# Input loads of a fused FFT-mixing and ELU kernel: row cuts, gather spacing, the read of channel 128

## The chip, the core and the metric

The kernel runs on one core of one Trainium2 chip. The metric is the device time of one execution in microseconds; the median of three runs of the kernel before is 1978.52 us (1977.29 to 1978.53). Nothing else runs on the chip.

The core has five engines with an instruction stream each: PE (matmul), DVE (vector), ACT (activation functions, copies), POOL (general elementwise, gathers) and SP (issues DMAs). A DMA is issued by SP, ACT or POOL and carried out by the core's 16 DMA engines. An engine executes its stream in order, so an instruction that waits holds up all that stand behind it.

## The reference

```python
X = np.fft.fft(x, axis=1)          # x: (8, 3008, 256)
X = np.fft.fft(X, axis=2).real
h = X.reshape(24064, 256) @ w_in   # (256, 2048)
g = np.where(h > 0.0, h, np.exp(np.minimum(h, 0.0)) - 1.0)
out = g @ w_out                    # (2048, 256)
```

The real part of the two-dimensional transform of a real x is C x C' - S x S', with cosine and sine matrices along the sequence (C, S) and the channels. It is even under a flip of both axes. The kernel therefore transforms half of the sequence, 1504 columns a batch, and gets the rows k and 3008 - k of the output from the sum and the difference of the same two products. The transform along the channels is multiplied into w_in on the chip, once.

## The kernel before, in words

**Columns, tiles, steps.** There are 8 x 1504 = 12032 columns in 47 tiles of 256 (TW). A tile takes 8 steps, 376 in all; each step handles two blocks of 128 of the 2048 hidden channels. A batch is 47 steps. In a step PE computes P (`mm_P`, H<-Rr,Wc) and Q (`mm_Q`, H<-Ir,Ws), DVE adds channel 128 between them (`even_part`, L960, E<-Rb,wex,H), ACT and DVE form the ELU of h plus and h minus, POOL forms four sums of the results (`sum_1`, `sum_3`, `sum_2`, `sum_4`, all through `gtt`, L484), and PE multiplies by w_out in seven products (`mm_X1`, `mm_X2`, `mm_X3` into pA to pD; pB's second product, from WT, needs `sum_2`). The first two tiles use the plain form without sums, since POOL is then converting weights. Results are transposed on DVE and stored by SP (`store`, L1191), up to 16 DMAs a transposed half.

**Input.** The sequence transform of a batch starts from folds: rows s, 3008 - s, 1504 - s and 1504 + s are brought onto the same partition, so that sums and differences can be formed (`fold_x`, L572: e0 to e3, o0 to o3, then E0, E2, EO0 and so on). `load_x` fills four tiles L[0] to L[3] (named xl) of 128 partitions x 6 rows of 256 channels. Each holds three pairs of rows, of which one kind runs forward at the pace of 8 rows a partition and comes by plain DMAs (`runs`, L238, queue SP, or ACT for most loads of the first batch), and the other is read backward through six gathers on POOL (`gather`, L217), whose row numbers stand in the table `ix` (`row_tables`, L189). The table RUNS cuts the 128 partitions where the row number jumps: at 96, 94 or 64. In the last batch one gather is followed by a repair (L228) of one row that would lie past the end of x; it is issued on POOL into the same tile.

**The rest of the start.** Weights come as 64-bit floats and are converted on DVE, ACT and POOL in chunks (`Chunk`: a, b, p, l, d, R, s, M, P are its operations; raw loads at L283), and folded with the channel transform on PE (f0 and so on). `load_mats` brings the transform matrices MC. PE starts with 46 matmuls on zeros.

**Channel 128** has no partner in the flip and is treated apart: `load_ext` (L806) reads it for all batches, 4 bytes a row, in 50 DMAs, already sorted into the order of the folds, through a DRAM tensor (xe_dr, L829) and back over 128 partitions (`get_ext`, L837: tile xs); `fold_ext` (POOL) and `dft_ext` (PE, H<-MC,xe) follow, and `spread_ext` broadcasts the result to Rb. `spread_last_row` (L524, L527) sends the matching row of each weight chunk through DRAM into wex.

**Order.** The order of most work on each engine is written out by hand: `at(t, fn)` puts a piece at a planned time, in units where a step is T = 4.8, and all pieces are issued in the order of t; FRONT lists the pieces of the first steps by name. What is wrapped in `pin` keeps this order on its engine. Plain DMAs outside `pin` are placed on their queue by a planner, by when their data are ready in its own estimate. SP's DMAs use eight semaphores in turn (the trace shows the numbers 100, 102 and 104 to 109): one that reuses a semaphore waits until the DMA before on it has landed. Each of the tiles xl has one buffer, so a load of the next batch waits until the folds have read the last one.

**Lines that the change touches:** RUNS (L120), `row_tables` (L175), `gather` (L211), `runs` (L232), the list of loads (L243), the entry `ops["x1", 0]` of `fold_x`, `load_ext` and `get_ext`, the first calls after the warm-up matmuls, and the times of `load_ext`, `get_ext` and the gathers:

```python
for n in range(24):
    at((14.4 + 0.33 * n) * T, lambda n=n: load_ext(*divmod(n, 6)))
at(30.0 * T, get_ext)
...
    l0, gap = (s0 - 8, 1) if b > 1 else (3.2, 0.5)      # s0 = 47 (b - 1)
    t = l0 + gap * n / 1.5 if n < 6 else l0             # gather n of batch b
```

Of the kernel before, what the change touches and what calls it, by code (L numbers as in the profile page):

```python
# [9 lines left out]
FP = mybir.dt.float32  # L10
# [5 lines left out]
ALU = mybir.AluOpType  # L16

SEQ = 3008
ND = 256
# [92 lines left out]
def _pick_consts():  # L112
# [6 lines left out]

RUNS = (  # L120
    (0, 0, 96, 0, 8),
# [9 lines left out]
def kernel(  # L131
# [42 lines left out]

    def row_tables():  # L175

        for c, first, n, base in (
            (1, 0, 128, 750),
            (1, 96, 32, 250),
            (0, 0, 128, HALF - 1),  # L180
            (0, 96, 32, HALF - 501),
            (2, 0, 128, HALF - 5),
            (2, 64, 64, HALF - 259),
            (3, 0, 128, HALF - 1),
            (3, 96, 32, HALF - 501),
            (3, 0, 1, HALF - 2),
        ):
            pin(
                nc.gpsimd.iota(  # L189
                    ix[first : first + n, c : c + 1],  # L190
                    pattern=[[0, 1]],
                    base=base,
                    channel_multiplier=-8,
                )
            )
            if c == 1 and first:
                pin(
                    nc.vector.tensor_scalar(
                        out=ix[:, 1:2], in0=ix[:, 1:2], scalar1=0x3FF, scalar2=None,
                        op0=ALU.bitwise_and,  # L200
                    )
                )

    def load_x(b):

        L = [
            spool.tile([128, 6 * ND], FP, tag=f"xl{j}", bufs=1, name=f"xl{j}")
            for j in range(4)
        ]

        def gather(j, pair):  # L211
            back = j in (1, 2)
            cut = b == NB - 1 and j == 1 and pair == 0
            c = 3 if cut else pair
            block = 2 - pair if back else pair
            pin(
                nc.gpsimd.indirect_dma_start(  # L217
                    out=L[j][:, 2 * block * ND : (2 * block + 2) * ND],
                    out_offset=None,
                    in_=xflat,  # L220
                    in_offset=bass.IndirectOffsetOnAxis(
                        ap=ix[:, c : c + 1].bitcast(U32), axis=0
                    ),
                    element_offset=(b * SEQ + (HALF if j in (1, 3) else 0)) * ND,
                )
            )
            if cut:
                nc.gpsimd.dma_start(  # L228
                    out=L[1][0:1, 4 * ND : 5 * ND], in_=xrows(b, SEQ - 1, 1, 1, 1)
                )  # L230

        def runs(j, queue=nc.sync):  # L232
            back = j in (1, 2)
            for pair, p, q, r, step in RUNS:
                if back != (pair == 1):
                    continue
                row = (0, SEQ, HALF, HALF)[j] + (-r - 1 if back else r)
                queue.dma_start(  # L238
                    out=L[j][p:q, 2 * pair * ND : (2 * pair + 2) * ND],
                    in_=xrows(b, row, 8, q - p),  # L240
                )

        loads = [  # L243
            lambda j=j, pair=pair: gather(j, pair)
            for j, pair in ((3, 1), (2, 0), (2, 2), (0, 1), (1, 0), (1, 2))
        ]
        loads += [lambda j=j, **kw: runs(j, **kw) for j in (3, 2, 0, 1)]
        return L, loads
# [213 lines left out]
    nc.vector.memset(zero, 0.0)  # L462
    row_tables()
    r128_dr = dpool.tile([NB, HALF], FP, tag="r128", name="r128")
# [100 lines left out]

    def fold_x(L, engine_of, cuts_of):

# [12 lines left out]
        for j in range(4):  # L580
# [21 lines left out]
            O.append(o)  # L602
        ops["x1", 0] = lambda: act(L[1][0:1, 5 * ND :], L[0][0:1, 0:ND])
        op("E0", E[0], E[0], E[1], ALU.add)
# [188 lines left out]

    def load_ext(j, run):
        if j == 0 and run == 0:
            state["x1"] = spool.tile([128, HALF + 1], FP, tag="rx", bufs=1, name="x1")
        t = state["x1"][j * NB : (j + 1) * NB, 0:768].rearrange(
            "b (p m) -> b p m", m=6
        )
        pair, p, q, s, step = RUNS[run]  # L800
        back = j in (1, 2)
        row = (0, SEQ, HALF, HALF)[j] + (-s if back else s)

        def copy(m, p, q, row):
            pin(
                nc.sync.dma_start(  # L806
                    out=t[:, p:q, m : m + 1],
                    in_=bass.AP(
                        tensor=xt,
                        offset=x.offset + row * ND + 128,  # L810
                        ap=[
                            [SEQ * ND, NB],
                            [(-step if back else step) * ND, q - p],
                            [1, 1],
                        ],
                    ),
                )
            )

        with nc.allow_non_contiguous_dma(reason="one channel"):  # L820
            for o in range(2):
                first = row + (-o if back else o)
                if first == SEQ:
                    copy(0, 0, 1, 0)
                    copy(0, 1, q, first - step)
                else:
                    copy(2 * pair + o, p, q, first)
        if run == len(RUNS) - 1:
            nc.sync.dma_start(  # L829
                out=xe_dr[j], in_=state["x1"][j * NB : (j + 1) * NB, 0:768]  # L830
            )

    def get_ext():
        xs = state["xs"] = spool.tile([128, 4, NB, 6], FP, tag="xs", bufs=1, name="xs")
        with nc.allow_non_contiguous_dma(reason="short runs"):
            for j in range(4):
                nc.sync.dma_start(  # L837
                    out=xs[:, j], in_=xe_dr[j].rearrange("b (p m) -> p b m", m=6)
                )

# [418 lines left out]
    L_first, loads = load_x(0)  # L1259
    for load in loads[:7]:  # L1260
        load()
    for load in loads[7:]:
        load(queue=nc.scalar)
    exp_neg(warm)
    w1_chunks[0].load()
    nc.sync.dma_start(out=CC, in_=CC_dr.ap())
# [270 lines left out]
    def begin_folds(b):  # L1537
        state["EO"], state["ops"] = fold_x(
            state["L"], lambda key: nc.gpsimd, lambda key, n: (0, n) if n == 128 else (0, n // 2, n)
        )  # L1540
# [7 lines left out]
    at(11 * T + 3.6, lambda: spread_ext(0, 1))  # L1548
    for n in range(24):
        at(  # L1550
            (14.4 + 0.33 * n) * T,
            lambda n=n: load_ext(*divmod(n, 6)),
        )
    at(30.0 * T, get_ext)
    at(32 * T + 1.35, fold_ext)
# [11 lines left out]
    for b in range(1, NB):  # L1567
        s0 = (b - 1) * steps_b
        late = 2 if b == 1 else 0
        l0, gap = (s0 - 8, 1) if b > 1 else (3.2, 0.5)  # L1570
        if b > 1:
            at(l0 * T + 0.1, lambda b=b: open_x(b))
        for n in range(10):
            t = l0 + gap * n / 1.5 if n < 6 else l0
            if b > 1:
# [74 lines left out]
```

## Time and profile before

| | |
|---|---|
| median of three runs | 1978.52 us |
| the profiled execution | 1980.33 us, its span 1978.5 us |
| PE busy | 1935.5 us (98%) |
| POOL, DVE, ACT busy | 1403.5, 1316.0, 862.6 us |
| granted PE clock, whole span; 15.3 to 35.6 us | 0.99; 0.50 |
| DMA | 69.69 MB; 262269 packets, of which 245534 under 512 bytes |
| first P matmul (step 0) | 43.15 us |
| steps 0 to 375 | the rest, about 5.1 us each |

Times are from the start of the span. A row of a group of instructions names line, engine, operation, output<-input and count. "L475", "L481", "L484" and "L487" are the helpers through which every matmul, DVE tensor operation, POOL operation and ACT function goes, so these are told apart by their tiles. The idle time at the end of a row is that of the engine ahead of the instruction, with what ended it. The busy time of PE includes the warm-up and the matmuls at half clock. A queue named SPq or ACTq shows issue time, not transfer; where several issues are merged into one row, its duration includes the waits between them.

### The profile page before, as it was taken

To read this page: it belongs to the slowest core of one execution; us is meant where nothing else is said; L and a number is where in the kernel's file an instruction comes from. 1 tells how busy PE (TensorE), PEld (TensorE's weight loads), DVE (VectorE), ACT (ScalarE), POOL (GpSimd) and SP (SyncE) were. 2 spreads that over 40 slices of the span, in tenths; PEclk is the share of its full clock that TensorE was granted. 3 is DMA by queue.
4 is the path that set the end of the run, shared out by engine and by line. 5 is a ranking of instruction groups with operands and counts; after the bars stand their busy time and mean duration, and the time that the engine had idled before them with its cause. 6 is when DMAs were issued, how large, how long until landed. Compare 5 with 4: busy or idle time off the path is not lost.

```text
span 1978.5 us, 27318 instructions
## 1 busy us (share of the span) xinstructions
PE 1935.5 (98%) x8912; PEld 1656.1 (84%) x8912; DVE 1316.0 (67%) x2517; ACT 862.6 (44%) x1671; POOL 1403.5 (71%) x1869
## 2 busy tenths in 40 slices
PE   6999999999999999999999999999999999999999
PEld 3788778888888888888888888888878888888887
DVE  5876566667666666667666666666656666667666
ACT  2654344444444443444444444444434444444443
POOL 2788666787678776887677776778766787555665
PEclk7999999999999999999999999999999999999999
DMA  8315320110111111111111112102020000100101
GB/s 265 93 21 31 40 60 14 28 47 16 43 16 36 33 21 48 17 40 22 30 43 20 34 22 50 22 19 50 14 54 11 20 15 19 19 11 12 22 9 24
DMA packets 262269, 69.69 MB, mean 35 GB/s; under 512 B 245534, under 2 KB 246450, under 8 KB 262128
## 3 DMA queue, kind: packets, MB, share of 16 engines
q1 hardware_dynamic: 255496, 54.06, 14.6%
q0 software_dynamic: 3872, 12.59, 2.0%
q10 hardware_dynamic: 2760, 1.31, 0.3%
q8 instruction: 70, 1.15, 0.3%
q14 instruction: 71, 0.58, 0.1%
HBM read 43.07 MB, written 24.80 MB: 34 GB/s over the span
## 4 chain that ended last, share of the span: by engine, by line
PE 88%; DVE 4%; DMA 3%; POOL 2%; SPq 1%; issue 1%; ACT 0%; ACTq 0%; DVEq 0%; POOLq 0%
PE H L475 35%; PE pC L475 15%; PE pB L475 15%; PE pD L475 15%; PE pA L475 8%; DMA xl<-in_x_dram 2%; POOL G L484 2%; SPq L1191 1%; DVE G L990 1%; DVE E L960 1%; POOL xl L217 0%; DVE bs L481 0%; DVE v L481 0%; DMA wx<-Ws 0%; DVE u L481 0%
## 5 line engine op out<-in xcount | busy, mean ns | idle before, releaser
L484 POOL TENSOR_TENSOR G<-G 128x256 f32<-128x256 f32 x1440 | 1035.5, 728 | 494.2 <-DVE G L990 382.5
L960 DVE SCALAR_TENSOR_TENSOR E<-Rb,wex,H 128x256 f32<-128x256 f32 x752 | 328.0, 478 | 529.7 <-PE H L475 522.8
L487 ACT ACTIVATE G<-H 128x512 f32<-128x512 f32 x376 | 224.5, 597 | 976.9 <-DVE G L974 971.0
L475 PE MATMUL H<-Ir,Ws 128*128 128x256 f32 x1504 | 389.4, 381 | 5.6 <-DVE E L960 4.7
L475 PE MATMUL H<-Rr,Wc 128*128 128x256 f32 x1504 | 387.5, 380 | 3.0 <-DVE Ir L481 2.0
L475 PE MATMUL pC<-G,WT 128*128 128x256 f32 x1440 | 371.1, 380 | 0.0
L475 PEld LDWEIGHTS H<-Rr,Wc 128*128 128x128 f32 x1504 | 284.8, 190 | 54.5 <-issue 5.3
L475 PEld LDWEIGHTS H<-Ir,Ws 128*128 128x128 f32 x1504 | 279.2, 190 | 56.0 <-DVE E L960 9.3
L475 PEld LDWEIGHTS pC<-G,WT 128*128 128x128 f32 x1440 | 274.8, 191 | 37.7
L974 DVE SCALAR_TENSOR_TENSOR G<-E,H 128x512 f32<-128x512 f32 x376 | 257.2, 684 | 55.8 <-POOL G L484 13.6
L990 DVE SCALAR_TENSOR_TENSOR G<-G,H 128x512 f32<-128x512 f32 x376 | 256.1, 681 | 43.1 <-ACT G L487 42.9
L990 DVE SCALAR_TENSOR_TENSOR G<-M,G 128x512 f32<-128x512 f32 x376 | 257.1, 684 | 0.4 <-ACT M L487 0.4
L487 ACT ACTIVATE G<-G 128x512 f32<-128x512 f32 x376 | 233.3, 620 | 0.0
L475 PE MATMUL pA<-G,w 128*128 128x256 f32 x784 | 229.3, 379 | 0.0
L475 PE MATMUL pB<-G,w 128*128 128x256 f32 x784 | 229.3, 379 | 0.0
L475 PE MATMUL pD<-G,w 128*128 128x256 f32 x784 | 229.3, 379 | 0.0
L475 PE MATMUL pB<-G,WT 128*128 128x256 f32 x720 | 216.8, 383 | 10.0 <-POOL G L484 9.7
L487 ACT ACTIVATE M<-G 128x512 f32<-128x512 f32 x376 | 224.3, 596 | 3.3 <-DVE G L974 3.3
L487 ACT ACTIVATE M<-M 128x512 f32<-128x512 f32 x376 | 221.0, 588 | 0.1
L475 PE MATMUL pD<-G,WT 128*128 128x256 f32 x720 | 214.6, 380 | 0.0
L475 PEld LDWEIGHTS pD<-G,w 128*128 128x128 f32 x784 | 149.1, 190 | 20.3
L475 PEld LDWEIGHTS pA<-G,w 128*128 128x128 f32 x784 | 148.9, 190 | 20.5
(170 smaller groups left out, 1455.1 us busy)
## 6 DMA issues: line engine op xcount, KB each, us to landing
out_dram<-ot SPq DMA_DIRECT2D x496, 32.0 KB
out_dram<-ot SPq DMA_DIRECT2D x256, 2.0 KB
xl<-in_x_dram SPq DMA_DIRECT2D x30, 128.0 KB
Rb<-r SPq DMA_DIRECT2D x10, 376.0 KB
raw<-in_moe_w_in_dram SPq DMA_DIRECT2D x7, 512.0 KB
xl<-in_x_dram SPq DMA_DIRECT2D x15, 192.0 KB
xl<-in_x_dram SPq DMA_DIRECT2D x14, 188.0 KB
raw<-in_moe_w_out_dram SPq DMA_DIRECT2D x4, 512.0 KB
```

Of the source, the lines that this page charges most:

```text
L475: nc.tensor.matmul(out_, lhsT=lhsT, rhs=rhs, start=start, stop=stop, skip_group_check=True)
L484: pin(nc.gpsimd.tensor_tensor(out=o, in0=a, in1=b, op=op))
L487: pin(nc.scalar.activation(out=o, in_=i, func=func, **kw))
L960: nc.vector.scalar_tensor_tensor(out=S.E[:, c], in0=Rb[:, cols(i)], scalar=wex[:, f : f + 1], in1=S.H[:, c], op0=ALU.mult, op1=ALU.add,)
L974: nc.vector.scalar_tensor_tensor(out=two(S.G[:, 0:512])[:, :, ::-1], in0=two(S.E), scalar=2.0, in1=two(S.H), op0=ALU.mult, op1=ALU.subtract,)
L990: nc.vector.scalar_tensor_tensor(out=o, in0=e, scalar=-1.0, in1=h, op0=ALU.add, op1=ALU.max)
L1191: queue.dma_start(out=bass.AP(tensor=out.tensor, offset=out.offset + r0 * ND + half * 128 + 32 * g, ap=[[2 * ND, w], [64 * ND, nb], [1, 32 ...
```

## The change

- **Cuts of the plain loads.** `runs` gives way to `ahead` (tiles 0 and 3: both forward pairs in one DMA, 64 + 32 + 32 partitions) and `back` (tiles 1 and 2: 96 + 32 partitions, for tile 1 80 + 14 + 34). A batch has 11 plain loads instead of 12. All are issued on SP; in the first batch eight of them were on ACT.
- **Order at the start.** The row table of the first gather is made alone, then come this gather, the plain loads of tile 3 and weight chunk 0, then two more tables, the other gathers and loads; the table for the last batch is last.
- **Gathers of batches 2 to 7** stand one step apart instead of two thirds of a step.
- **The repair load** of the last batch is replaced by a copy on ACT, of a row that the same tile already has (`first_row`).
- **Channel 128** is read in natural row order, four DMAs for each of four parts and one more, into a tile of its own (xn) from step 10.2 on, 0.7 of a step apart; six ACT copies (`sort_ext`, at 24T + 1.5) sort it; one DMA writes it to DRAM, and one (`get_ext`, at 26T) brings it back.

```diff
-RUNS = (
+EXT_RUNS = (
...
         def gather(j, pair):
             back = j in (1, 2)
-            cut = b == NB - 1 and j == 1 and pair == 0
-            c = 3 if cut else pair
+            c = 3 if b == NB - 1 and j == 1 and pair == 0 else pair
...
-            if cut:
-                nc.gpsimd.dma_start(
-                    out=L[1][0:1, 4 * ND : 5 * ND], in_=xrows(b, SEQ - 1, 1, 1, 1)
-                )
-
-        def runs(j, queue=nc.sync):
-            back = j in (1, 2)
-            for pair, p, q, r, step in RUNS:
-                if back != (pair == 1):
-                    continue
-                row = (0, SEQ, HALF, HALF)[j] + (-r - 1 if back else r)
-                queue.dma_start(
-                    out=L[j][p:q, 2 * pair * ND : (2 * pair + 2) * ND],
-                    in_=xrows(b, row, 8, q - p),
+
+        def ahead(j):
+            pairs = L[j].rearrange("p (m c) -> p m c", c=2 * ND)[:, 0::2]
+            for p, q, row, gap in ((0, 64, 0, 4), (64, 96, 512, -254), (96, 128, 500, 14)):
+                nc.sync.dma_start(
+                    out=pairs[p:q],
+                    in_=bass.AP(
+                        tensor=xt,
+                        offset=x.offset + (b * SEQ + (HALF if j else 0) + row) * ND,
+                        ap=[[8 * ND, q - p], [gap * ND, 2], [1, 2 * ND]],
+                    ),
+                )
+
+        def back(j):
+            last = (SEQ if j == 1 else HALF) - 1
+            cuts = (0, 80, 94, 128) if j == 1 else (0, 96, 128)
+            for p, q in zip(cuts, cuts[1:]):
+                s = 750 - 8 * p if p < 94 else 1018 - 8 * p
+                nc.sync.dma_start(
+                    out=L[j][p:q, 2 * ND : 4 * ND], in_=xrows(b, last - s, 8, q - p)
                 )
...
-        loads += [lambda j=j, **kw: runs(j, **kw) for j in (3, 2, 0, 1)]
+        loads += [
+            lambda: ahead(3), lambda: back(2), lambda: ahead(0), lambda: back(1)
+        ]
...
-        ops["x1", 0] = lambda: act(L[1][0:1, 5 * ND :], L[0][0:1, 0:ND])
+
+        def first_row():
+
+            if last:
+                act(L[1][0:1, 4 * ND : 5 * ND], L[1][0:1, 5 * ND :])
+            act(L[1][0:1, 5 * ND :], L[0][0:1, 0:ND])
+
+        ops["x1", 0] = first_row
...
+    def load_ext(j, k):
+        if j == 0 and k == 0:
+            state["x1"] = spool.tile([128, 776], FP, tag="xn", bufs=1, name="x1")
+        t = state["x1"][j * NB : (j + 1) * NB]
+
+        def copy(s0, s1, row, step):
+            pin(
+                nc.sync.dma_start(
+                    out=t[:, s0:s1],
                     in_=bass.AP(
                         tensor=xt,
                         offset=x.offset + row * ND + 128,
+                        ap=[[SEQ * ND, NB], [step * ND, s1 - s0], [1, 1]],
                     ),
                 )
             )
 
+        s0, s1 = 192 * k, 192 * k + 192
...
+    def sort_ext():
+
+        src = state["x1"][0 : 4 * NB]
+        t = spool.tile([128, HALF + 1], FP, tag="rx", bufs=1, name="xp")
+        t = t[0 : 4 * NB, 0:768]
+        dst = t.rearrange("q (p m) -> q p m", m=6)
+        for pair, p, q, s, step in EXT_RUNS:
+            n = q - p
+            low = s if step > 0 else s + step * (n - 1)
+            rows = src[:, low : low + 8 * n].rearrange("q (n e) -> q n e", e=8)[:, :, 0:2]
+            act(dst[:, p:q, 2 * pair : 2 * pair + 2], rows if step > 0 else rows[:, ::-1])
+        nc.sync.dma_start(out=xe_dr.rearrange("j b r -> (j b) r"), in_=t)
 
     def get_ext():
         xs = state["xs"] = spool.tile([128, 4, NB, 6], FP, tag="xs", bufs=1, name="xs")
         with nc.allow_non_contiguous_dma(reason="short runs"):
-            for j in range(4):
-                nc.sync.dma_start(
-                    out=xs[:, j], in_=xe_dr[j].rearrange("b (p m) -> p b m", m=6)
-                )
+            nc.sync.dma_start(
+                out=xs.rearrange("p j b m -> p (j b) m"),
+                in_=xe_dr.rearrange("j b (p m) -> p (j b) m", m=6),
+            )
...
     L_first, loads = load_x(0)
-    for load in loads[:7]:
+    row_table(1)
+    loads[0]()
+    loads[6]()
+    w1_chunks[0].load()
+    row_table(0)
+    row_table(2)
+    for load in loads[1:6] + loads[7:]:
         load()
-    for load in loads[7:]:
-        load(queue=nc.scalar)
+    row_table(3)
     exp_neg(warm)
-    w1_chunks[0].load()
...
-    for n in range(24):
-        at(
-            (14.4 + 0.33 * n) * T,
-            lambda n=n: load_ext(*divmod(n, 6)),
-        )
-    at(30.0 * T, get_ext)
+    for n in range(16):
+        at((10.2 + 0.7 * n) * T, lambda n=n: load_ext(*divmod(n, 4)))
+    at(24 * T + 1.5, sort_ext)
+    at(26 * T, get_ext)
...
-        l0, gap = (s0 - 8, 1) if b > 1 else (3.2, 0.5)
+        l0 = s0 - 8
...
-            t = l0 + gap * n / 1.5 if n < 6 else l0
+            t = l0 + n if n < 6 else l0
```

More of the change, by code (lines that the diff above doesn't have):

```diff
@@ L173, with row_table @@
     ix = cpool.tile([128, 4], I32, tag="ix")
[L175 to L187, printed above, removed]
+    def row_table(c):
+        for first, n, base in (
+            ((0, 128, HALF - 1), (96, 32, HALF - 501)),
+            ((0, 128, 750), (96, 32, 250)),
+            ((0, 128, HALF - 5), (64, 64, HALF - 259)),
+            ((0, 128, HALF - 1), (96, 32, HALF - 501), (0, 1, HALF - 2)),
+        )[c]:
             pin(
@@ L195, in row_tables @@
             )
[L196 to L200, printed above, removed]
-                    )
+        if c == 1:
+            pin(
+                nc.vector.tensor_scalar(
+                    out=ix[:, 1:2], in0=ix[:, 1:2], scalar1=0x3FF, scalar2=None,
+                    op0=ALU.bitwise_and,
                 )
+            )
     def load_x(b):
@@ L462 @@
     nc.vector.memset(zero, 0.0)
-    row_tables()
     r128_dr = dpool.tile([NB, HALF], FP, tag="r128", name="r128")
@@ L563, in sum_weights, with fold_x @@
         gtt(W[3], W[1], b21, ALU.add)
-    def fold_x(L, engine_of, cuts_of):
+    def fold_x(L, engine_of, cuts_of, last=False):
         ops = {}
@@ L791, in half @@
                 vtt(R4b, self.es[:, 0:1], self.odd[:, 0:1], ALU.subtract)
[L794 to L798, printed above, removed]
-        )
[L800 to L804, printed above, removed]
+    def load_ext(j, k):
[3 more added lines that the diff above has]
+        def copy(s0, s1, row, step):
             pin(
                 nc.sync.dma_start(
-                    out=t[:, p:q, m : m + 1],
+                    out=t[:, s0:s1],
                     in_=bass.AP(
@@ L810, in copy @@
                         offset=x.offset + row * ND + 128,
[L811 to L815, printed above, removed]
+                        ap=[[SEQ * ND, NB], [step * ND, s1 - s0], [1, 1]],
                     ),
@@ L818, in copy @@
             )
+        s0, s1 = 192 * k, 192 * k + 192
         with nc.allow_non_contiguous_dma(reason="one channel"):
[L821 to L828, printed above, removed]
-            nc.sync.dma_start(
-                out=xe_dr[j], in_=state["x1"][j * NB : (j + 1) * NB, 0:768]
-            )
+            if j == 1 and k == 0:
+                copy(0, 1, 0, 1)
+                copy(1, s1, SEQ - 1, -1)
+            else:
+                step = -1 if j in (1, 2) else 1
+                copy(s0, s1, (0, SEQ, HALF, HALF)[j] + step * s0, step)
+    def sort_ext():
[9 more added lines that the diff above has]
+        nc.sync.dma_start(out=xe_dr.rearrange("j b r -> (j b) r"), in_=t)
     def get_ext():
@@ L835, in get_ext @@
         with nc.allow_non_contiguous_dma(reason="short runs"):
-            for j in range(4):
-                nc.sync.dma_start(
-                    out=xs[:, j], in_=xe_dr[j].rearrange("b (p m) -> p b m", m=6)
-                )
+            nc.sync.dma_start(
+                out=xs.rearrange("p j b m -> p (j b) m"),
+                in_=xe_dr.rearrange("j b (p m) -> p (j b) m", m=6),
+            )
     def fold_ext():
@@ L1538, in begin_folds @@
         state["EO"], state["ops"] = fold_x(
-            state["L"], lambda key: nc.gpsimd, lambda key, n: (0, n) if n == 128 else (0, n // 2, n)
+            state["L"],
+            lambda key: nc.gpsimd,
+            lambda key, n: (0, n) if n == 128 else (0, n // 2, n),
+            b == NB - 1,
         )
@@ L1548 @@
     at(11 * T + 3.6, lambda: spread_ext(0, 1))
-    for n in range(24):
-        at(
-            (14.4 + 0.33 * n) * T,
-            lambda n=n: load_ext(*divmod(n, 6)),
-        )
-    at(30.0 * T, get_ext)
+    for n in range(16):
+        at((10.2 + 0.7 * n) * T, lambda n=n: load_ext(*divmod(n, 4)))
+    at(24 * T + 1.5, sort_ext)
+    at(26 * T, get_ext)
     at(32 * T + 1.35, fold_ext)
```

## The prediction

> **What bounds the kernel now.** I read the page's first part, then who waited for whom on PE, then the chain of waits over the first 50 us, then timelines and stretches round each wait.
>
> ```profile
> PE 1935.5 (98%) x8912; PEld 1656.1 (84%) x8912; DVE 1316.0 (67%) x2517; ACT 862.6 (44%) x1671; POOL 1403.5 (71%) x1869
> ```
> PE bounds the span: 1978.5 - 1935.5 = 43 us idle. So a change to loads can win only idle PE time, plus what happens before the first real step (43.1 us, the first H<-Rr,Wc matmul), where the 46 warm-up matmuls (12.1 us) and half-clock matmuls count as busy. The waits on PE (columns: total us, times, longest):
> ```profile
> PE H L475 <- DVE w L369: 10.7, 1, 10.7
> PE pB L475 <- POOL G L484: 9.7, 14, 4.0
> PE H L475 <- DVE E L960: 4.7, 5, 2.4
> PE H L475 <- POOL xe L484: 4.2, 1, 4.2
> PE pC L475 <- DVE xe L481: 2.9, 1, 2.9
> ```
> The first and last are the start, and its chain (start us, us, what) is one buffer:
> ```profile
> 1.98 18.03 DMA xl<-in_x_dram
> ...
> 20.03 9.81 DMA xl<-in_x_dram
> ...
> 29.96 0.17 DVE xa L481
> ```
> These are two of the eight input loads on ACT's queue, end to end. Yet the engines of the DMA are not full (last columns: granted PE clock, DMA share, GB/s):
> ```profile
> 10.00:14.00 4.00, 3.20 (x15) 1.26 (x13) 1.83 (x2) 0.00 (x0) 0.15 (x1) 1.00 1.03 346
> 16.00:18.00 2.00, 0.00 (x0) 0.00 (x0) 0.67 (x2) 0.00 (x0) 0.00 (x0) 0.50 0.17 54
> 18.00:20.00 2.00, 0.00 (x0) 0.00 (x0) 0.79 (x2) 0.00 (x0) 0.00 (x0) 0.50 0.21 78
> ```
> A share of 0.17 to 0.21 is some three engines of 16: few engines are late, not the memory. ACT, which issues those loads, does nothing else meanwhile:
> ```profile
> 0.75 19.52 ACTq L238 DMA_DIRECT2D xl<-in_x_dram  x8
> 20.30 1.28 ACT L487 ACT_TABLE_LOAD   x1 [20.30 <-DMA xl<-in_x_dram]
> 21.70 0.70 ACT L487 ACTIVATE pow<-pow,ebias 128x512 int32<-128x512 int32 x1
> ```
> The 4.2 us wait is channel 128: its last quarter is read on SP behind 48 stores, and POOL waits for it.
> ```profile
> 206.09 23.43 SPq L1191 DMA_DIRECT2D out_dram<-ot  x48
> 229.56 0.43 SPq L837 DMA_DIRECT2D xs<-xe_dr  x1
> 231.87 0.38 POOL L484 TENSOR_TENSOR xs<-xs 128x96 f32<-128x96 f32 x1 [5.15 <-DMA xs<-xe_dr]
> ```
> The pB waits are gathers between POOL's sums (first three lines), once with the repair behind its gather (last three):
> ```profile
> 515.58 0.96 POOL L217 DMA_INDIRECT xl<-in_x_dram,ix  x1
> 516.56 2.35 POOL L484 TENSOR_TENSOR G<-G 128x256 f32<-128x256 f32 x3
> 518.15 0.70 PE L475 MATMUL pB<-G,WT 128*128 128x256 f32 x2 [0.47 <-POOL G L484]
> ...
> 1475.61 0.55 POOL L228 DMA_DIRECT2D xl<-in_x_dram  x1 [2.95 <-DMA xl<-in_x_dram,ix]
> 1476.18 2.34 POOL L484 TENSOR_TENSOR G<-G 128x256 f32<-128x256 f32 x3
> 1477.78 1.22 PE L475 MATMUL pB<-G,WT 128*128 128x256 f32 x2 [3.97 <-POOL G L484]
> ```
>
> [...] the 94-row load's semaphore jumps at 1.40 us and gets its last two counts at 10.64 and 12.57; a 96-row load has 14 counts by 3.17 and the last two at 4.29 and 5.53[...] The trace has 0.50 from 15.3 to 35.6 us, while DVE sets the pace.
>
> **A, start.** Removed: the 94/34 cuts, 2 x (94 + 34) rows x 2 KB on two engines = 256 KB each; at 84 ns a 2 KB packet (the trace's median) 128 x 0.084 = 10.8 us alone, with their shares of everything else until 29.84. Left on two engines: one 34-row load, 17 x 0.084 = 1.4 us. Everything before the weights' rest is x 3.08 MB, w_in chunk 0.52, CC and MC 0.90: 4.5 MB; at the 330 GB/s or so of 6 to 14 us that is 13.6 + 2 = 15.6 us. Then DVE sets the order. First gather: two iotas end near 1.2 instead of 2.5, so it issues at 1.6 instead of 2.72. Four iotas at 0.2 us then move between it and the second: issues at 3.8, 5.1, 6.3, 7.6, 8.8. Landing takes 3.4 us where nothing is in the way (79.16 to 82.53), 8.5 to 9.7 at the start of before; I take 5 (bounds 3.4 and 8). e3 starts near 6.8 (before: 11.59), e3 and o3 1.8, w0's three 1.5, ACT's pow hidden in them (ACT is free from 1 us, its table loaded), w0s and w0M 1.4: 11.5. Then seven folds, 23.78 to 28.87 in before = 5.1: 16.6, with L0 and L2 landed by 11.5 and L1 by 14. Add 0.7 for slips: fold_first at 17.3 instead of 29.96: 12.7 us earlier. From there to step 0 DVE is dense in before (29.96 to 43.1), and I move that piece whole. Late next are the matrices MC10: behind about 8.7 MB at 390 GB/s (the rate at 36 to 44 us is 398) = 22 + 2 = 24.4, needed at 38.95 - 12.7 = 26.2. **A = 12.7** (bounds 6 and 14).
>
> **B, wex.** [...] at 61.01 it took 5.16 us behind a 94-row load, and PE waited 1.23 at 69.24. That load is gone: **1.2** (0 to 2).
>
> **C, channel 128.** 50 one-channel reads (35.6 us of SP in all), four writes and four reads become 17, one and one. The elements stay about 24,060 of 4 bytes; the mean issue of 0.73 us for some 490 elements becomes at most 2.3 for 1536, so 17 cost 12 to 39 us of SP; I take 25. The read of xs now stands at step 26, ahead of the 48 stores and 6 steps (30 us) ahead of its use: **C = 4.2**. The DVE burst behind it (3.6 us of PE waits, 244 to 258) stays.
> New costs. On ACT six copies of 32 partitions: 128x6 takes 0.20 and 32x375 0.51, so 64 to 192 elements 0.25 to 0.35, 1.8 us. They stand at 24T + 1.5, between x+ and x-; behind them wait x-, then DVE's g-, POOL's sums, PE's pB. ACT has some 2.3 us free in a step, and a gather of 0.96 in POOL's order cost 0.47: **1.0** (0 to 2). On SP the reads now begin at 10.2T, ahead of the last wex spread (13.04T). Its E already waited for it in before (1.10 us on DVE at 134.86, none on PE); one or two more issues and up to 3 us of landing: **1.5** (0 to 4).
>
> **D, gathers.** At 2/3 of a step the second and fifth of a batch stand at 0.7 of a step, between POOL's sums 1 and 3; the first and fourth, before sum 4, cost PE nothing. Whole steps put all six there. PE's pB waits at those places (281, 293, 518, 530, 754, 766, 990, 1003, 1238, 1462) add up to 0.66 + 0.46 + 0.46 + 0.47 + 0.47 + 0.40 + 0.47 + 0.41 + 0.40 + 0.80: **5.0** (3 to 5.2). The sixth gather is 1.7 steps later, still two steps before the folds.
>
> **E, repair.** POOL's 2.95 wait and 0.55 issue go: **4.0**. The added ACT copy (0.40) hides under ACT's idle half; uncovered it costs 0.4. Eleven loads for twelve on SP in each later batch count as nothing: they land during the steps of the batch before, and no PE wait ends on them.
>
> Sum: 12.7 + 1.2 + 4.2 + 5.0 + 4.0 - 2.5 = 24.6. The profiled execution took 1980.33 us, its span 1978.5; after: span 1953.9, with the same 1.8 around it 1955.7. The median of the runs, 1978.52, lies 1.8 under the profiled one, so 1953.9; I say 1954.
>
> **Rivals.** (1) *The start moves only in part*: gathers land 8 us after issue beside a full SP queue, or MC10 and the chunks come late, and A is 6 to 7: 1960. For it: PE at half clock, SP in-order; against it: DMA at 0.2 share from 16 to 22 us. (2) *The wait moves to ACT*: ACT, in order, waits in the sort for a read still stuck on SP behind stores; C is given back and 2 to 6 us more: 1958 to 1964. Against it: about three steps between the last read (20.7T) and the sort. (3) *The spacing does nothing*, as POOL's order was not the cause: 1959. (4) *Slower*: SP. If each of the 17 reads holds SP for more than about 4.8 us, they do not fit in the 74 us from step 10 to 24 beside 20 us of stores and spreads (17 x 4.8 + 20 = 102, 28 over), and the sort on ACT turns the overrun into PE time; at 5.2 us each it is 34 over, 1988. For it: single issues up to 2.39 us; against it: the mean is 0.73.
>
> **Chances.** Forecast 0.66 (1948 to 1960), (1) 0.18, (2) 0.07, (3) 0.04, (4) 0.05, of which 0.02 within 0.2% (4 us, about what a measurement can tell from no change). The range 1948 to 1964 leaves out (4), the ends of (1) and (2) and the tails of the forecast. Faster 0.95, same 0.02, slower 0.03.
>
> **What would show it.** A: ACT's table load near 1 us, fold_first near 17, step 0 near 30.5, no stretch of 0.2 share before it. B: wx lands in under 2 us. C: no PE wait on xe near step 32; ACT's first sort copy not waiting for a DMA. D: no pB waits of 0.4 to 0.8 at gathers. E: no POOL wait in the last batch. I am wrong if step 0 starts after 35, or ACT or DVE shows a new wait on SP's DMAs between 90 and 180 us.

## The result: 1962.5 us, and a ratio of 0.992

The changed kernel takes 1962.51 us (median of four runs, 1957.26 to 1964.17) against 1977.9 us of the kernel before (now the median of four, 1976.69 to 1978.53): a ratio of 0.9918, 95% interval 0.9898 to 0.9938. It is faster, by 15.4 us where 24.6 were forecast: inside the range of 1948 to 1964 that the prediction gave, but above the 1948 to 1960 that it gave its own forecast. The profiled executions show the same: span 1978.5 before, 1962.4 after, 16.1 less (their own times are 1980.33 and 1964.17 us).

The first part of the page of the changed kernel, and its list of who waited for whom on PE (total us, times, longest):
```profile
PE 1929.7 (98%) x8912; PEld 1655.8 (84%) x8912; DVE 1310.3 (67%) x2517; ACT 864.3 (44%) x1678; POOL 1403.9 (72%) x1868
```
```profile
PE H L476 <- DVE E L968: 12.2, 6, 5.2
PE H L476 <- DMA CC<-chan_mats: 5.9, 1, 5.9
...
PE pB L476 <- POOL G L485: 0.7, 3, 0.3
```
The 10.7 us of before at the start and the 4.2 for channel 128 are gone, and the pB waits fell from 9.7 to 0.7. But the waits for E, which is DVE's addition of channel 128, rose from 4.7 to 12.2. Two of these waits are new or longer. To see what each stretch gained, I took the start of the first P matmul of each step from both traces and formed differences:

| stretch (steps) | before, us | after, us | difference |
|---|---|---|---|
| start to step 0 (A) | 43.15 | 35.2 | -7.95 |
| 4 to 8 (B: weight rows, first batch) | 31.0 | 34.5 | +3.5 |
| 14 to 16 (the last wex) | 10.4 | 17.0 | +6.6 |
| 32 to 34 (C: channel 128) | 18.0 | 11.7 | -6.3 |
| 40-60, 80-100, 120-140, 180-200, 220-240: gathers but for the last batch (D) | 521.6 | 515.1 | -6.5 |
| 260 to 280 (D and E, last batch) | 114.1 | 106.6 | -7.5 |
| step 360 to the end | 89.2 | 91.0 | +1.8 |

The rest is within 0.3 a row. The last row is no effect of the change: among the twelve runs below, nearly all of whose code there is the same, it took 89.1 to 91.1 us.

**The two waits.** SP's timeline of the changed kernel round 60 us (start, duration), then what DVE and PE did (the bracket is the idle time in front of the instruction and what ended it):
```profile
53.06 0.22 SPq L525 DMA_DIRECT2D wx<-Ws  x1
53.45 0.39 SPq L285 DMA_DIRECT2D raw<-in_moe_w_in_dram  x1
60.23 0.39 SPq L285 DMA_DIRECT2D raw<-in_moe_w_out_dram  x1
60.71 0.42 SPq L528 DMA_DIRECT2D wex<-wx  x1
```
```profile
64.31 0.87 DVE L968 SCALAR_TENSOR_TENSOR E<-Rb,wex,H 128x256 f32<-128x256 f32 x2 [6.73 <-DMA wex<-wx]
...
134.62 0.87 DVE L968 SCALAR_TENSOR_TENSOR E<-Rb,wex,H 128x256 f32<-128x256 f32 x2 [5.02 <-DMA wex<-wx]
```
```profile
65.24 2.07 PE L476 MATMUL H<-Ir,Ws 128*128 128x256 f32 x4 [5.17 <-DVE E L968]
...
135.54 2.08 PE L476 MATMUL H<-Ir,Ws 128*128 128x256 f32 x4 [3.29 <-DVE E L968]
```
A weight load (chunk 6 of w_out) stands between the two halves of the spread of one weight row. Its buffer is free only when POOL has converted what is in it, at 60.23; so it waits, and the second half (wex<-wx), whose data had been there since 54.16, waits behind it in SP's order. In the kernel before the two halves stood in front of that load (66.18 and 68.17). The wait at 135.54 is the last spread of this kind, which now stands behind three reads of channel 128; DVE waited 1.10 us for it in the kernel before, and PE not at all.

**The half clock.** The same four matmuls H<-Ir,Ws take 1.03 us elsewhere and 2.07 here. The view by stretches (columns: span, busy time of PE, PEld, DVE, ACT, POOL; then granted PE clock, DMA share, GB/s) of the changed kernel shows why:
```profile
56.00:63.00 7.00, 4.07 (x20) 3.28 (x18) 1.57 (x3) 4.51 (x9) 5.45 (x7) 1.00 0.32 80
63.50:70.00 6.50, 4.76 (x11) 3.83 (x12) 5.05 (x12) 1.73 (x3) 1.68 (x2) 0.50 0.30 81
71.00:78.00 7.00, 7.00 (x35) 5.56 (x32) 4.64 (x8) 4.67 (x10) 3.62 (x4) 1.00 0.27 75
```
From 63.26 to 70.08 PE ran at half clock: it did 11 matmuls in 6.5 us, where 35 fit in 7. In the traces of before and after the granted clock changes only at times that lie a multiple of 3.41 us apart, and the stretches at 0.50 last that long or a multiple of it (3.4 or 6.8 us, 20.5 at the start of before), unless the trace ends in one. I took both window by window on this grid, from 44 to 1900 us. At full clock, all seven windows in which PE was idle for 59% or more (59, 69, 70 and 71% in before, 69, 79 and 93% in after) were followed by one at half clock; none of the others was, in which PE was idle for 53% at most. The waits in the seven were of 2.01, 3.97, 4.19 and 2.35 us in before and of 2.36, 3.29 and 5.17 in after. Of the ten windows at half clock, the three in which PE was idle for 18, 48 and 58% were followed by another; the seven with 7% at most were not.

So such a wait costs more than the idle time in its row, by up to half of the stretch at half clock that is busy. Idle time plus half of the part of the stretch that lies behind the wait (an estimate from the two traces) gives 7.6 us for the 5.17, 6.4 for the 3.29 and 5.9 for the 4.2 of channel 128 in before; the steps round them changed by 7.8 (as experiment 1 shows), 6.6 and 6.3. The 4.0 of the repair stood in a stretch worth 7.5.

### The profile page after: what moved, and what is told of

Its sections match the earlier page's. It is cut to its first block, busy times and chain, and to the rows that moved or that the text cites. A ratio compares the mean times of both kernels' runs of the same rounds, so it can differ in the third digit from the quotient of the medians.

```text
span 1962.4 us, 27279 instructions
## 1 busy us (share of the span) xinstructions
PE 1929.7 (98%) x8912; PEld 1655.8 (84%) x8912; DVE 1310.3 (67%) x2517; ACT 864.3 (44%) x1678; POOL 1403.9 (72%) x1868
## 4 chain that ended last, share of the span: by engine, by line
PE 93%; DVE 4%; DMA 1%; POOL 1%; issue 1%; SPq 0%; ACT 0%; DVEq 0%; POOLq 0%
PE H L476 37%; PE pB L476 16%; PE pC L476 16%; PE pD L476 16%; PE pA L476 8%; DVE E L968 1%; DVE G L998 1%; POOL G L485 0%; DMA xl<-in_x_dram 0%; DMA CC<-chan_mats 0%; DVE v L482 0%; DVE bs L482 0%; DVE e L573 0%; DMA wex<-wx 0%; DVE u L482 0%
## 5 line engine op out<-in xcount | busy, mean ns | idle before, releaser
L476 PE MATMUL H<-Ir,Ws 128*128 128x256 f32 x1504 | 390.0, 382 | 13.1 <-DVE E L968 12.2
L476 PEld LDWEIGHTS pB<-G,w 128*128 128x128 f32 x784 | 151.3, 193 | 21.3
```

Of the source, the lines that this page charges most:

```text
L476: nc.tensor.matmul(out_, lhsT=lhsT, rhs=rhs, start=start, stop=stop, skip_group_check=True)
```

## Experiments

All ratios are to the kernel before on the same chip, and all differences of stretches are between profiled executions.

### 1. The weight load behind the spread, the reads later, and both

One load is pinned at its written place, so that it stays behind the spread:
```diff
-        def load(self):
+        def load(self, keep=False):
...
-            nc.sync.dma_start(
+            d = nc.sync.dma_start(
                 out=words.rearrange("p (a b) -> p a b", a=n), in_=self.src.bitcast(I32)
             )
+            if keep:
+                pin(d)
...
-        at(t * T, chunk.load)
+        at(t * T, lambda chunk=chunk: chunk.load(chunk is w2_chunks[6]))
```


> One weight load (chunk 6 of w_out), which stands on SP's queue ahead of the wex read of chunk 2 and waits there for POOL, is kept at its written time, behind that read. Theory (head of line): the PE wait of 5.17 us at 65 us goes to about 1 us or less, and the half clock from 63.3 to 70.1 us, which costs another 3.4, goes with it: 7 to 8 us faster than the changed kernel, 1955. Rival (POOL is late anyway, and the wait is moved): a wait of 3 us or more is still there between 55 and 75 us, and the time stays within 2 us of 1962.5.

In the second, the reads of channel 128 begin behind the last spread (13.04T):
```diff
-        at((10.2 + 0.7 * n) * T, lambda n=n: load_ext(*divmod(n, 4)))
-    at(24 * T + 1.5, sort_ext)
-    at(26 * T, get_ext)
+        at((13.1 + 0.68 * n) * T, lambda n=n: load_ext(*divmod(n, 4)))
+    at(25 * T + 1.5, sort_ext)
+    at(26.9 * T, get_ext)
```


> The channel 128 reads start at 13.1T instead of 10.2T, so behind the wex spread of chunk 7; sort and read back come one step later. Theory (the reads delay wex): the PE wait of 3.29 us at 135.5 us and the half clock from 134.9 to 141.8 us go: 6 to 7 us faster than the changed kernel, 1956. Rival (the broadcast to Rb, which stood there before the change too, delays wex): the wait stays above 2 us, no change beyond 1.5 us. If the sort on ACT then waits for reads, a new wait appears near step 25.

> Both edits. If the two waits are separate, the gains add: 13 to 15 us faster than the changed kernel, 1948 to 1950, and no run to run spread from half clock windows after stalls. If removing one wait lets the other grow, less than 10 us.

Measured: the pinned load gives 1951.99 us, ratio 0.9852 (0.9821 to 0.9883), span 1950.3; the late reads 1962.2 us, 0.9918 (0.989 to 0.9947); both 1955.02 us, 0.9871 (0.9835 to 0.9908).

SP's timeline with the pinned load:
```profile
52.35 0.22 SPq L527 DMA_DIRECT2D wx<-Ws  x1
...
53.56 0.39 SPq L530 DMA_DIRECT2D wex<-wx  x1
```
The second half goes out at 53.56 instead of 60.71, there is no PE wait near 65 us (the granted clock is 1.00 from 62 to 70 us), and steps 4 to 6 take 11.7 us instead of 19.5: -7.8. The place of one load on SP's queue cost about half as much as the whole change won. The rest of the 12.1 us between the spans lies in a start 0.7 earlier, a tail 1.9 shorter, two shorter stretches near 130 and 250 us (1.4 and 1.7; from 134 to 142 us the granted clock was 1.00, in the changed kernel 0.57) and a loss of 1.4 at steps 24 to 26. The first four differ from one execution to the next. The loss is the sort, here at the time that the change gave it:
```profile
178.97 1.37 ACT L490 ACTIVATE xp<-x 32x192 f32<-32x192 f32 x6 [2.71 <-DMA x<-in_x_dram]
```
In the changed kernel the same copies waited 1.36 us, and steps 24 to 26 took 9.6 us. Eight of the profiled kernels have the sort at this time. Where it waited up to 1.5 us, the two steps took 9.5 to 9.7; in the four where it waited 2.3 to 2.9, they took 10.6 to 11.2. So the sort is free only while the last read lands in time.

With the late reads the wait at 135 us was gone too (steps 14 to 16: 10.4 us), but the time stayed. ACT's timeline in that run says where it went:
```profile
190.72 1.35 ACT L488 ACTIVATE xp<-x 32x192 f32<-32x192 f32 x6 [5.77 <-DMA xl<-in_x_dram]
```
The first copy of the sort waits for the last reads. Behind it on ACT stands M<-M of the ELU, and DVE's sum of it, which PE needs: it waited 5.00 us at 193.33. (The row names a DMA into xl, but the copies read only the tile of channel 128, whose last read was on SP until 183.7. One semaphore tells of DMAs of different tiles: in the changed kernel number 104 does so for a load of xl issued at 43.64 us and for wx at 53.06. So the name is probably that of a neighbour.) Steps 26 to 28 took 17.0 us instead of 9.5. This is rival (2) in full, brought about by my own timing: +7.5, for -6.6 gained at 14 to 16. In the kernel with both edits the same wait stood at 184.76, so the gains did not add.

### 2. The sort two steps later

```diff
-    at(25 * T + 1.5, sort_ext)
-    at(26.9 * T, get_ext)
+    at(27 * T + 1.5, sort_ext)
+    at(29 * T, get_ext)
```


> e3_both with the sort on ACT two steps later (27T + 1.5) and its spread and read back two steps later too (29T); nothing else. In e3_both the sort stood in ACT's order at 182.2 us and waited 5.12 us for the last one-channel read, which cost PE a wait of 4.35 us and 6.8 us at half clock: the two steps took 17.0 us instead of 9.5. Theory (the sort's place was the only reason that the gains of e1_wex_ahead and e2_ext_late did not add): the wait and its half clock go, -7.5 us on e3_both's profile, 1946 to 1947.5 us. Rival (the reads of 4-byte elements themselves take away what they free, somewhere else on SP's queue): a new wait on an SP transfer after step 20, and no more than -3 us.

Measured: 1952.8 us, 0.9857 (0.9835 to 0.988), span 1950.8: 3.0 less than with both edits, not 7.5. Steps 26 to 28 are back at 9.5, so the sort's wait was a matter of its place. But SP and POOL now show:
```profile
188.58 23.35 SPq L1201 DMA_DIRECT2D out_dram<-ot  x48
211.97 0.42 SPq L846 DMA_DIRECT2D xs<-xe_dr  x1
```
```profile
216.27 0.39 POOL L487 TENSOR_TENSOR xs<-xs 128x96 f32<-128x96 f32 x1 [3.69 <-DMA xs<-xe_dr]
```
At 29T the read back stands behind 48 stores, just as in the kernel before, and PE waits 2.74 us for it at 217.08, with 3.4 us at half clock: steps 32 to 34 took 16.6 us instead of 11.7. The rival's prediction of a new SP wait came true, but from the read back, not from the one-channel reads. It also tests C the other way round: what removes the wait of before is that the read back is ahead of the stores.

So there is room between the two: the sort after the last read, the read back before the stores.
```diff
-    at(29 * T, get_ext)
+    at(27.5 * T, get_ext)
```


> e9_both_sort_late with the spread and the read back at 27.5T, behind one store instead of behind all 48; the sort stays where e9 has it. In e9 the read back stood in SP's order behind 23.35 us of stores and POOL waited 3.69 us for it, PE 2.74 and then 3.4 us at half clock: the two steps from 32 on took 16.6 us instead of 11.7. Expected: neither the sort's wait (e3) nor this one, so 1950.8 - 4.9 = 1946 us in the profile, ratio near 0.983. If the reads themselves cost what they free, some other wait of over 2 us appears and the time stays above 1949.

Measured: 1946.99 us (1945.76 to 1948.14), 0.9846 (0.9823 to 0.9869), span 1944.9, the fastest kernel of the study. Steps 26 to 28 take 9.5, 32 to 34 11.7, 14 to 16 10.4. PE's waits in it:
```profile
PE H L478 <- DVE E L970: 3.7, 4, 2.4
```
The one longer wait in the list, 6.0 us, ended at 18.6 us while DVE sets the pace of the start. After step 0 the longest is 2.36 us, one that before had too. With these orders the change is worth 1978.5 - 1944.9 = 33.6 us of span, against 16.1 as it came (by the ratios, 30 and 16 us).

### 3. The start: cuts or order

The old order, with ACT's queue for most loads, but the new cuts:
```diff
-    row_table(1)
-    loads[0]()
-    loads[6]()
-    w1_chunks[0].load()
-    row_table(0)
-    row_table(2)
-    for load in loads[1:6] + loads[7:]:
+    for c in (1, 0, 2, 3):
+        row_table(c)
+    for load in loads[:7]:
         load()
-    row_table(3)
+    for load in loads[7:]:
+        load(queue=nc.scalar)
     exp_neg(warm)
+    w1_chunks[0].load()
```


> The changed kernel with its new cuts, but the start issued as in the kernel before: four row tables first, six gathers, then the plain loads of tiles 2, 0 and 1 on ACT's queue, ACT's table and the first weight chunk after them. Prediction's step A split in two: if the cuts (no load on two engines) were the gain, the last plain load of tile 0 still lands near 17 and step 0 starts within 1.5 us of the changed kernel's 35.2, or later by the 3 to 4 us by which ACT's table and the weight chunk come late; if the order was the gain, step 0 goes back to 40 to 43. I expect step 0 at 37 to 39, time +2 to +4 us on the changed kernel's.

And the new order, but the old cuts:
```diff
-            cuts = (0, 80, 94, 128) if j == 1 else (0, 96, 128)
+            cuts = (0, 94, 128)
```


> The changed kernel with its new order, but the two backward loads of each batch cut at row 94 again, as in the kernel before: two engines carry 4 times 128 to 188 KB of 2 KB packets. At the 84 to 136 ns that such a packet took, the 128 packets that each of the two engines must carry for them are 11 to 17 us beside their share of all else, so the last row of tile 0 or 1 lands at 22 to 28: step 0 at 40 to 44, time +5 to +9 us, and the wait for the spread weight rows grows as before (+1 us). Rival: the rate of all engines together sets the landing near 17; then step 0 stays within 1 us of 35.2.

| cuts, order | step 0 at, us | time, us | ratio |
|---|---|---|---|
| old, old (before) | 43.15 | 1977.9 | 1 |
| new, old | 34.0 | 1954.3 | 0.9865 (0.9845 to 0.9885) |
| old, new | 41.3 | 1969.53 | 0.9938 (0.9918 to 0.9959) |
| new, new (after) | 35.2 | 1962.51 | 0.9918 (0.9898 to 0.9938) |

The cuts alone are worth 9.1 us at step 0, the order 1.9 on the old cuts and nothing on the new (35.2 in this execution, 33.0 to 35.1 in the seven other full kernels that have both, mean of the eight 34.1). With the old cuts DVE waits for tile x as the prediction had it for before:
```profile
21.53 1.02 DVE L573 TENSOR_TENSOR e<-xl 128x512 f32<-128x512 f32 x2 [8.29 <-DMA xl<-in_x_dram]
```
A load of xl that was issued at 7.24 us landed 20.50 us later here, and the DMA share falls to 0.63 between 16 and 22 us, where it is 0.95 in the changed kernel. That such loads run on two engines is an estimate from the trace of before: from 17 to 19 us its DMA share is 0.13, two engines of 16, and the semaphore of its 34-row load, issued at 1.34, moves three times only, at 1.76, 16.66 and 18.33 us, as that of its 94-row load does, while that of a load of 96, 64 or 32 rows moves sixteen times. In the changed kernel the 80-row load moves its own sixteen times and lands at 18.66; one 34-row load is left, and it lands at 18.52. Later PE waits 6.46 us for the spread, at 73 us, instead of 5.17. Both are as expected. The time, expected 5 to 9 us longer than the changed kernel's, is 6.7 longer by the spans and 4.0 by the ratios.

What I had wrong is the kernel with the old order: I expected it slower than the changed one by 2 to 4 us, and it is faster (ratio 0.9865 against 0.9918). At the start the two differ by 1.2; but steps 4 to 6 take 11.7 us instead of 19.5. SP's timeline:
```profile
53.77 0.39 SPq L529 DMA_DIRECT2D wex<-wx  x1
59.06 0.39 SPq L286 DMA_DIRECT2D raw<-in_moe_w_out_dram  x1
```
The w_out load is behind the spread again. Nothing at 50 us was edited; the planner placed an unpinned load differently because the start differed. So the new order of the start is what brought the 5.17 us wait, and it bought nothing for it.

To see whether the order is worth anything once the spread is safe, I put the old one into the fastest kernel:

> e12_sort_between with the start issued as in the kernel before (as e5_old_start_order). In e5 that order alone took the changed kernel to 0.9865, with step 0 at 34.0 instead of 35.2 and the spread of a weight row ahead of the w_out load, which e12 has by other means. If the order at the start has no worth of its own, e13 is within 2 us of e12, with step 0 at 33 to 35 in both; if it is worth what e5 showed beside the spread, e13 is 1 to 4 us faster.

Measured: 1947.74 us, 0.9851 (0.9829 to 0.9874), beside 1946.99 and 0.9846 on the same chip, step 0 at 34.0 and 33.6. The order at the start has no worth of its own that shows.

### 4. Why the input came late

Step A had the input of tile 0 by 11.5 us. DVE's timeline of the changed kernel:
```profile
17.01 1.03 DVE L573 TENSOR_TENSOR e<-xl 128x512 f32<-128x512 f32 x2 [4.47 <-DMA xl<-in_x_dram]
```
The first fold started at 7.96, 1.2 us after my 6.8, and those of tile 0 at 17.01, 5.5 late. It was not a few engines that were late: the share of all 16 was 1.04 from 8 to 16 us, and the rate was low, 250 GB/s. In these two runs the six gathers of batch 0 give way to plain loads of the same bytes into the same places, on ACT's queue or on POOL's. Within each of these loads the rows stand in rising order, so the input of batch 0 is in the wrong order and the output with it; the work and the bytes are the same. Each kernel was executed once.
```diff
+            if b == 0:
...
+                    nc.scalar.dma_start(
+                        out=L[j][p : p + n, 2 * block * ND : (2 * block + 2) * ND],
+                        in_=bass.AP(
+                            tensor=xt,
+                            offset=x.offset + (row - 8 * (n - 1) + (HALF if j in (1, 3) else 0)) * ND,
+                            ap=[[8 * ND, n], [1, 2 * ND]],
+                        ),
+                    )
+                return
```


> The changed kernel, but the six gathers of batch 0 are plain loads on ACT's queue that bring the same bytes to the same places, with the rows of each in rising order (so batch 0's input is in the wrong order; the work and the amount of data are the same). ACT's table is loaded ahead of them. Question: why the input of step A landed at 16.9 and not near 12. Theory (loads by the gathers slow the mix: 250 ns for 4 KB and 136 ns for 2 KB packets between 8 and 16 us, where 84 is the least): the rate of 2 to 16 us rises from about 250 to 330 GB/s or more, the last plain load of tile 0 lands by 14, and step 0 starts at 31 to 33. Rival (the start's loads share what 16 engines give, whoever describes them): the rate stays within 10% of 250 GB/s, the landing within 1.5 us of 16.9, and step 0 within 1.5 us of 35.

> As e10_start_plain_ascending, but those plain loads are issued by POOL in the gathers' places (again batch 0's rows are in rising order within each load). If a list of row addresses is what makes the gathers slow, the landing is that of e10; if POOL's queue is, whatever it carries, rate and landing are those of the changed kernel (250 GB/s, 16.9, step 0 near 35).

The stretch from 8 to 16 us, in the changed kernel, then with plain loads on ACT's queue, then on POOL's (last three columns: PE clock, DMA share, GB/s):
```profile
8.00:16.00 8.00, 5.31 (x25) 2.17 (x23) 4.47 (x7) 0.83 (x2) 2.22 (x5) 0.97 1.04 250
```
```profile
8.00:16.00 8.00, 5.72 (x27) 2.34 (x24) 3.06 (x6) 0.82 (x2) 0.00 (x0) 1.00 1.04 245
```
```profile
8.00:16.00 8.00, 5.97 (x28) 2.47 (x26) 4.49 (x7) 0.83 (x2) 3.50 (x9) 1.00 1.06 232
```
The rate does not rise without gathers, whoever issues (from 2 to 8 us too: 254, 263 and 259); the fastest kernel, with the same start, has 269 GB/s from 8 to 16 us. Step 0 stood at 34.8 and 35.6; the first of these says little alone, since ACT was busy with its issues and DVE waited for ACT's pow until 14.98. The rate decides: the gathers are not the cause. (The times of the two, 1961.46 and 1954.12 us, differ mostly at steps 4 to 6, 20.0 and 11.7 us: in the second the w_out load stands behind the spread again, though only the loads of the start were edited.)

The rate that I had used was wrong. From 8 to 16 us the kernel before moved 331 GB/s, but by the numbers and sizes of its packets that was 1.3 MB of weights and matrices, 1.1 of gathers and only 0.2 of plain loads of x. In the same trace the stretch from 2 to 8 us gave 214 GB/s. And with the old order and the new cuts, from 2 to 8 and from 8 to 16 us, it is
```profile
2.00:8.00 6.00, 6.00 (x20) 2.29 (x19) 0.00 (x0) 0.07 (x1) 4.45 (x8) 1.00 0.99 243
8.00:16.00 8.00, 5.79 (x28) 2.41 (x26) 4.54 (x8) 2.25 (x4) 1.84 (x2) 1.00 1.05 323
```
low while the plain loads of x run and high when gathers and matrices follow. So stretches in which these loads prevail run at 214 GB/s (before, 2 to 8 us) to 269 (the fastest kernel, 8 to 16 us) here, at a DMA share of 0.80 to 1.06. Why, no run shows; that stays open.

Of the 5.5 us by which tile 0 came late, the rate explains about 3.5: from 2 to 17 us 3.8 MB moved, which at 330 GB/s would have ended at 13.5 (an estimate from these figures). The rest is the order: 11.5 us at that rate stands for 3.1 MB moved by the end of tile 0, and it was 3.8.

### 5. The gathers' spacing and the repair

The spacing back at two thirds:
```diff
-            t = l0 + n if n < 6 else l0
+            t = l0 + n / 1.5 if n < 6 else l0
```


> The changed kernel with gathers two thirds of a step apart again. Theory (POOL order): ten pB waits of 0.4 to 0.8 us come back at the second and fifth gather of a batch: 5.0 us slower than the changed kernel; by the step times of the two traces up to 6.6. Rival (the spacing does nothing): within 1 us, and no pB waits.

The repair row loaded again, at the new spacing:
```diff
+            if c == 3:
+                nc.gpsimd.dma_start(
+                    out=L[1][0:1, 4 * ND : 5 * ND], in_=xrows(b, SEQ - 1, 1, 1, 1)
+                )
...
-            if last:
-                act(L[1][0:1, 4 * ND : 5 * ND], L[1][0:1, 5 * ND :])
```


> The changed kernel with the repair row of the last batch loaded by POOL's DMA behind its gather again, without the copy on ACT. Prediction's step E: PE waits 4.0 us near 1460, and the time is +4.0 us. If a wait of this length also leaves PE at half clock, as the traces of before (6.8 us after 1476) and after (6.8 us after 65 and 135) show, it is +5.7 to +7.4 us.

Two thirds gave 1970.62 us, 0.995 (0.993 to 0.9969): 6.3 us more than the changed kernel by the ratios, 7.8 by the spans, as expected. PE's waits for the sums are back, in the same places as before:
```profile
PE pB L476 <- POOL G L485: 6.7, 15, 0.8
```
The repair load gave 1960.1 us, 0.9899 (0.9877 to 0.9921): no slower than the changed kernel, where I had expected at least 4.0 us more. For the stretch of steps 260 to 280 this is the full table, in us:

| | spacing two thirds | spacing one step |
|---|---|---|
| repair by a load | 114.1 (before) | 106.8 |
| repair by a copy | 108.1 | 106.6 (after) |

POOL's timeline at the repair, at the new spacing:
```profile
1461.18 0.96 POOL L211 DMA_INDIRECT xl<-in_x_dram,ix  x1 [0.15 <-issue]
1464.82 0.55 POOL L222 DMA_DIRECT2D xl<-in_x_dram  x1 [2.68 <-DMA xl<-in_x_dram,ix]
1465.39 2.92 POOL L489 TENSOR_TENSOR G<-G 128x256 f32<-128x256 f32 x4
```
POOL still waits 2.68 us for the gather, but with a whole group of sums before it (at 1458.13) and a whole group behind, at a point where nobody needs the next sum yet: PE shows no wait there. In before, the same pair stood behind the first sum of a step (1470.82) and in front of the other three (1476.18), and PE waited 3.97 us. So the spacing and the copy remove the same wait. Each does it alone: 7.3 us for the spacing, 6.0 for the copy, 7.5 for both.

## Why the prediction was right, and where it was not

The direction and the range held, and so did what bounds the kernel: only idle PE time and the time before step 0 were to be won. The sum missed by 8.5 us of span (24.6 forecast, 16.1 measured), and that it missed by no more is in part luck: A, B and the last wex came 14.5 us short, the tail took another 1.8, and C, D and E gave 8.1 more than forecast. Both signs that the prediction named for being wrong came true: step 0 started after 35, at 35.2, and DVE waited for an SP transfer between 90 and 180 us, 5.02 us for wex at 134.62, where it had been 1.10.

**A, forecast 12.7, measured 7.95** (9.1 for the cuts alone with the old order). The part with the two-engine loads is shown: on the new order, step 0 stood at 41.3 with the old cuts and at 35.2 with the new. The failed term is the landing of tile 0, at 11.5, for which I used 330 GB/s: it was 17.0, at 250. (The stretch that the 330 was said to be of, 6 to 14 us in before, reads 312.) fold_first came at 22.04 instead of 17.3. The piece from there to step 0, moved whole, took 13.1 us as in before. This is rival (1) in its size (6 to 7) more than the forecast; of its reasons, the late gathers were right (they landed 6.3 to 9.7 us after their issue), while the matrices were not what held DVE: from 17.01 us to step 0 it shows no wait above 0.4 us. The earlier gathers and the free ACT, which the step counted in, brought nothing: the old order does as well.

**B, forecast -1.2, measured +3.5.** The failed step is that I took only the wx transfer as late and left SP's order as it was. The wait for wx was gone (with the load pinned, the second half of the spread went out 1.2 us after the first). But a different start gave a different order at 50 to 60 us, and an unpinned load with a wait of its own came in front of wex. The prediction's last sentence had looked for such waits between 90 and 180 us; this one was at 65.

**The wex of the last chunk, forecast +1.5 (0 to 4), measured +6.6.** The place and cause were right. The size was off, because half clock was not in it: 3.29 us idle, then 6.8 us at half clock.

**C, forecast -4.2 and +1.0 for the sort, measured -6.3 and nothing.** The read back ahead of the stores removed the wait of 4.19 us, as said, and its 3.4 us of half clock as well. The six copies waited 1.36 us for a read and PE did not notice; in four of the other kernels with the same timing they waited 2.3 to 2.9 us and the two steps took 1.1 to 1.7 longer, so the nothing was partly luck, and the forecast of 1.0 (0 to 2) fair. The 17 reads took 20.2 us of SP where I took 25.

**D and E, forecast 5.0 and 4.0, measured 14.0 together.** The copy at the old spacing is worth 6.0, the spacing with the copy 7.9 over the steps of all gathers. As steps of the sum they were treated as independent, which they are not: of E only 0.2 is left after D (106.8 against 106.6). That the total is above the forecast all the same comes from the prices, which were the idle times of the rows. The 3.97 that ended at 1477.78 brought 6.8 us at half clock, so the last batch gave 7.5 instead of 4.8. And in the first four batches the steps shrank by 1.4 to 1.5 us where the rows of their pB waits show 0.9 to 1.1; no half clock is seen there, and the reason for that difference stays open.

**The rivals.** (2) did not happen in the profiled execution of the change, though ACT already waited 1.36 us; it showed in small in the four kernels above, and in full when the reads moved three steps later. (3) fell: the spacing matters. (4) fell: the reads took 1.2 us each. By its own numbers they would have stopped fitting at 3.2 us each, (74 - 20) / 17, and not at 4.8, which is where the whole gain would be lost.

## What to carry to other kernels

SP issues its DMAs in order, and even a small transfer can be on the critical path: here one load in front of the second half of a spread put its issue at 60.71 us instead of 53.56, and steps 4 to 6 took 19.5 us instead of 11.7. Before moving loads, list which waits of other instructions will stand in front of each short transfer on that queue, and pin the ones whose order matters, since a planner may reorder far from the edit. Look at the granted clock behind each PE wait: here those of 5.17, 3.29 and 4.19 us brought 0.50 for 3.4 or 6.8 us, and the steps round them changed by 7.8, 6.6 and 6.3 us, about the idle time plus half of the half-clock stretch that lay behind the wait. Add gains only where the edits do not remove the same wait, and take a transfer rate from a stretch that moves the same kind of load (with the old order and the new cuts it was 243 GB/s from 2 to 8 us and 323 from 8 to 16).

## What the runs showed of the hardware

- PE waits of 2.01 to 5.17 us were followed by a granted clock of 0.50 for 3.4 or 6.8 us: in before 2.01 (3.4 us), 4.19 (3.4), 2.35 (3.4) and 3.97 (6.8), in after 5.17 (6.8), 3.29 (6.8) and 2.36 (3.4), in the kernel with both edits 4.35 (6.8), with the sort two steps later 2.74 (3.4). The length of the wait alone did not set that of the stretch: 4.19 us brought 3.4, 3.29 brought 6.8. Nor is the time at half clock the same in each execution of a kernel: the granted clock of the four runs of the changed kernel was 0.993 to 0.996 on average, by estimate 27 to 16 us at 0.50 ((1 - clock) / 0.5 of the span).
- Replacing gathers by plain loads of the same bytes did not raise the rate of the start (250 GB/s from 8 to 16 us with them, 245 and 232 without), and the packets cost about the same by the byte: in the changed kernel, from 8 to 16 us, 252 ns for 4 KB and 136 ns for 2 KB (medians; the gathers move the 4 KB packets, the plain loads and a weight chunk those of 2 KB). The share of the DMA engines read 1.04 at 250 GB/s (the changed kernel) and 1.05 at 323 (the old order with the new cuts), both from 8 to 16 us, so a full share does not say what rate is had.
